# A planned attention and gated-MLP kernel: chunk 3's later score products added half to half, one denominator matmul for chunk 0, narrower last output pieces, and a new order

## The chip, the cores and the metric

The kernel runs on one core of one Trainium2 chip. Times are microseconds (us) on the device. The reported time is the median of several executions; one further execution was recorded by the profiler. An execution's time is a little longer than the span from the first to the last instruction that the profile shows.

The engines are named as the profile names them: PE multiplies matrices (PEld loads its weights), DVE works on vectors, ACT evaluates functions and copies out of PSUM, POOL and SP here mainly issue DMAs.

## The reference, cut to what matters

```python
h  = x + A(layernorm(x), wqkv, wo)           # x: [1, 2048, 512], bf16
h2 = h + B(layernorm(h), W_gate, W_up, W_down)

# A: 32 heads of 16, window of 8 keys at distance 0, 2, ..., 14 behind the query
logits = einsum("bhsd,bhswd->bhsw", q, kg) * scale     # masked where the key lies before position 0
attn   = softmax(logits, axis=-1)
o      = einsum("bhsw,bhswd->bhsd", attn, vg)
return o @ wo

# B: F = 1376
gate = relu(x @ W_gate);  up = x @ W_up
return (gate * up) @ W_down
```

## The kernel before

The 2048 rows go through in four chunks (0 to 3) of 512 columns. For each chunk a helper adds steps to a plan; each step has one engine, and a list `RANK` gives each step its place. `Plan.order` sorts every engine's steps by rank, so the list fixes the order in which each engine (and each DMA-issuing queue) takes its steps; steps of all four chunks are mixed. A step never overtakes another on its engine: when it waits, all behind it wait. `RANK` has one number per step in the order in which the steps are added, so a change that adds steps needs a new list.

The steps of one chunk `tk`, with the names used below:

- Layernorm of x: statistics (`xst`, `xag`, DVE, L467 and L470), Ln and Exp for the reciprocal root (ACT, L480, L484), normalising (L499 on ACT, L502 on DVE), transposing into columns by PE (L531, evacuated at L547) or by a transposing DMA on SP (L520, chunk 3).
- Projections q, k, v (PE, L572, four matmuls of 128x512 each; evacuated by ACT, L580).
- Products q*k: `pr` (DVE, L620, two head slices and four window positions in one instruction of 128x4096; chunk 0 in halves, L637). There are two half-windows hf = 0, 1, and for each two instructions, t = 0 and t = 2. One such tile has 8 slices of 512 columns: four window positions of head slice t, then the same four of slice t+1.
- Scores: `sc` (PE, L628). A matmul with the selector `sel` sums a head's elements over partitions, four of them side by side on 32 columns of the array. One `sc` step has 16 matmuls for the two tiles of a half-window. Then the exponential, `ex` (ACT, L696).
- Denominators: `den`. Chunks in `DEN1` first add the two half-windows' exponentials on DVE (`es`, L728) and use one matmul (L713); a chunk outside sums both in two matmuls (L716). Then Ln and Exp for the reciprocal (`dl`, `dr`, ACT, L719, L722). Chunks 1 to 3 multiply the weights by it early (`am`, DVE, L740).
- Broadcast of the weights to all elements of a head, `bd`: eight DMAs per chunk on SP (L756).
- Weighted values: `mu` (DVE, L788, 128x4096; chunk 0 in halves, L803), four per chunk, each followed by a tree of three additions. The first, 2048 wide, is an accumulating DMA issued on POOL for chunks 0 to 2 (`ta`, L831) and a DVE addition for chunk 3 (L791); the two others are on DVE (L791, L825).
- Output projection `wo0` to `wo3` (PE, L867), each needing all four trees; the residual (`rs`, DVE, L878; ACT for chunk 0), squares (ACT, L456), normalising (L502), transposes (PE, L531, or SP, L520).
- GLU: groups of four matmuls for up (`mmu`) and gate (`mmg`) per 128 features (PE, L940), evacuated by ACT (L944, L947), multiplied on DVE (`gu`, L968); the last 96 features go another way, in two tail groups (`mmT`, PE, L907; L913, L917).
- Down projection `dn` (PE, L990): 8 + 3 matmuls for 128 rows of output; then the residual (chunk 0 and 1: ACT copy L999 and accumulating DMA on POOL, L1024, `oa`; chunk 2 and 3: DVE, L1003) and the write (L1009, L1027, `os`). For chunk 3 the last 128 rows are done in column pieces cut at `LASTC`; the piece added last to the plan is written from ACT's queue, the others from SP's.

PSUM has eight banks of 128x512 in fp32, shared by all products of PE. PE begins with 56 matmuls on a zero tile (L421) and two smaller series of such (L429).

Of the kernel before, what the change touches and what calls it, by code (L numbers as in the profile page):

```python
# [17 lines left out]
RANK = [  # L18
# [38 lines left out]
]  # L57


# [33 lines left out]
class Plan:  # L93
# [9 lines left out]
    def add(self, key, *a, **k):  # L103
        op = Op(*a, **k)
        op.key = key
        op.seq = len(self.ops)
        if RANK:
            op.prio = RANK[op.seq]
        self.ops.append(op)
        for b in set(op.take) | set(op.use):  # L110
            b.left += 1
        return op
# [90 lines left out]
def kernel(  # L203
# [12 lines left out]
    Bsz, S, D = A_x.shape  # L216
# [5 lines left out]
    W = 8  # L222
    DIL = 2
    PADL = 16
    DEN1 = (1, 2, 3)
    BCD = {(0,0):"SSSS",(0,1):"SSSS",(1,0):"SSSS",(1,1):"SSSS",(2,0):"SSSS",(2,1):"SSSS",(3,0):"SSSS",(3,1):"SSSS"}
    PRE = ()
    PRD = ()
    PRH = {}
    ODA = (0, 1)  # L230
    LATE = "ud"
    NAB = 0
# [64 lines left out]
    V = nc.vector  # L297
# [94 lines left out]
    HSP = ()  # L392
    TMT = (0, 1, 2, 3)
    TTM, DTG, ATE = 0.0845, 0.35, 0.3
    LASTC = (D // 2,)

    LNA = ((0, 1, 0, 1), (0, 0, 0, 0))

# [156 lines left out]
    for tk in range(NCK):  # L555
# [50 lines left out]
        for hf in range(2):  # L606
            sc, ex = Buf(at_s), Buf(ex_s)
            scd, prd = [], []
            for t in range(0, NT, 2):
# [12 lines left out]

                hs = PRH.get((tk, hf, t))

# [62 lines left out]
            elif tk in MERGE:  # L687
                scd = [add(("sc%d" % hf, tk), "PE", (4 - sum((tk, hf, t) in PRH for t in (0, 2))) * MM + SW, lambda p=prd: [f() for _, _, f in p],
                           [a for a, _, _ in prd], apr, take=[sc], use=[b for _, b, _ in prd], lat=PEL)]
# [21 lines left out]
        def f_dn(exs=exs, dn=dn, tk=tk, es=None):  # L711
            if tk in DEN1:
                nc.tensor.matmul(dn.t[:], lhsT=(same if tk in EARLY else spread)[:], rhs=es.t[:], start=True, stop=True)  # L713
                return
            for hf in range(2):
                nc.tensor.matmul(dn.t[:], lhsT=(same if tk in EARLY else spread)[:], rhs=exs[hf].t[:], start=(hf == 0), stop=(hf == 1))  # L716
# [6 lines left out]

        if tk in DEN1:
            es = Buf(es_s)
# [250 lines left out]
        if tk == NCK - 1:  # L976
            cs = (0,) + LASTC + (D,)
            parts[-1:] = [(BPC - 1, a, b) for a, b in zip(cs, cs[1:])]
# [98 lines left out]
```

## Time and profile before

| | |
|---|---|
| median of 3 executions | 196.6 us (196.38 to 196.94) |
| profiled execution | 196.0 us |
| its span, first to last instruction | 193.7 us |
| PE busy | 188.5 us, 97% |
| DVE busy | 147.2 us, 76% |
| ACT busy | 115.2 us, 59% |
| POOL busy | 17.4 us, 9% |
| granted TensorE clock | 1.000 |

The profiled execution is 2.3 us longer than its span and 0.6 us shorter than the median. Busy time counts overlapping instructions once. A matmul of 128x512 shows a duration of 379 ns, but in a sequence the next one starts 216 ns after it, so lengths of sequences are read from the chain of waits, not from durations. The same holds, less strongly, for DVE and ACT.

### The profile page before, as it was taken

The numbers are of one execution on the slowest core, as the hardware profiler recorded it, in microseconds if no ns is written. First come the engines' busy times: TensorE is split into PE (matmuls) and PEld (weight loads), VectorE is DVE, ScalarE is ACT, GpSimd is POOL, SyncE is SP. The second block draws the span as 40 slices with busy tenths as digits, with TensorE's granted clock in tenths as the row PEclk, the third lists the DMA queues.
The fourth block names the chain that finished last, engine by engine and source line by source line (L and its number), as shares of the span: only waits on it lengthen the run. The fifth ranks groups of instructions, "written<-read, shape, count | busy, mean of one in ns | idle before, by whom it ended". The sixth has DMA issues, their size and how long they took to land.

```text
span 193.7 us, 3083 instructions
## 1 busy us (share of the span) xinstructions
PE 188.5 (97%) x1120; PEld 99.0 (51%) x1139; DVE 147.2 (76%) x239; ACT 115.2 (59%) x241; POOL 17.4 (9%) x35
## 2 busy tenths in 40 slices
PE   7999999999999999999999999999999999999993
PEld 7986455555436435454444554444445444545452
DVE  6889999999999999999997679999564401134331
ACT  3489898965999673965156649623478712435500
POOL 3000002330000013100044001003000000000000
PEclk9999999999999999999999999999999999999999
DMA  6799564999902609917579974135101624001102
GB/s 205 242 296 376 138 155 93 192 196 260 353 5 49 171 14 199 191 33 170 122 143 194 180 192 90 29 80 94 18 0 27 162 58 135 0 27 54 30 23 86
DMA packets 25070, 24.61 MB, mean 127 GB/s; under 512 B 11136, under 2 KB 21344, under 8 KB 25056
## 3 DMA queue, kind: packets, MB, share of 16 engines
q1 hardware_dynamic: 22032, 16.23, 30.1%
q0 software_dynamic: 2304, 7.34, 20.8%
q10 hardware_dynamic: 720, 0.85, 1.2%
q8 instruction: 9, 0.15, 0.3%
q14 instruction: 5, 0.04, 0.1%
HBM read 8.42 MB, written 2.10 MB: 54 GB/s over the span
## 4 chain that ended last, share of the span: by engine, by line
PE 97%; ACT 1%; issue 1%; DVE 0%; ACTq 0%
PE bank L940 35%; PE bank L572 21%; PE bank L990 20%; PE bank L867 7%; PE bank L628 4%; PE bank L421 3%; PE bank L907 3%; PE bank L531 2%; PE bank L429 1%; ACT up_sb L944 1%; PE bank L870 0%; PE bank L713 0%; PE bank L716 0%; DVE row L1003 0%; ACT vT L580 0%
## 5 line engine op out<-in xcount | busy, mean ns | idle before, releaser
L940 PE MATMUL bank<-quad,wgu_sb 128*128 128x512 bf16 x312 | 72.4, 379 | 0.4
L940 PEld LDWEIGHTS <-wgu_sb 128*128 128x128 bf16 x320 | 31.0, 98 | 36.4 <-issue 1.0
L990 PE MATMUL bank<-wd_sb,gT 128*128 128x512 bf16 (+2 forms) x185 | 39.6, 366 | 0.1
L944 ACT CAST up_sb<-bank 128x512 bf16<-128x512 f32 x40 | 22.3, 590 | 22.2 <-PE bank L940 20.5
L572 PE MATMUL bank<-quad,wqk_sb 128*128 128x512 bf16 (+1 forms) x148 | 29.4, 344 | 0.3
L947 ACT ACTIVATE gr<-bank 128x512 bf16<-128x512 f32 x40 | 23.5, 606 | 9.5 <-PE bank L940 5.2
L968 DVE TENSOR_TENSOR gT<-gr,up_sb 128x1024 bf16<-128x1024 bf16 x20 | 13.8, 688 | 19.4 <-ACT up_sb L944 10.5
L990 PEld LDWEIGHTS <-gT 128*128 128x128 bf16 (+1 forms) x187 | 18.2, 98 | 19.8 <-DVE gT L968 0.2
L620 DVE TENSOR_TENSOR big<-quad,kT 128x4096 bf16<-128x4096 bf16 x12 | 27.2, 2284 | 0.2 <-ACT kT L580 0.2
L788 DVE TENSOR_TENSOR big<-big,vT 128x4096 bf16<-128x4096 bf16 x12 | 27.1, 2285 | 0.2 <-PE bank L940 0.2
L572 PEld LDWEIGHTS <-wqk_sb 128*128 128x128 bf16 x152 | 16.7, 113 | 10.3 <-issue 0.2
L831 POOL DMA_DIRECT2D big<-big x12 | 10.5, 904 | 81.7 <-DVE big L788 54.2
L791 DVE TENSOR_TENSOR big<-big 128x1024 bf16<-128x1024 bf16 (+2 forms) x24 | 16.9, 728 | 0.0
L572 PE MATMUL bank<-quad,wv_sb 128*128 128x512 bf16 x61 | 15.3, 380 | 0.2
L867 PE MATMUL bank<-wo_sb,quad 128*128 128x512 bf16 x62 | 15.0, 379 | 0.1
L1003 DVE TENSOR_TENSOR row<-x_sm,bank 128x512 bf16<-128x512 bf16 (+1 forms) x9 | 5.5, 627 | 12.2 <-PE bank L990 12.2
L456 ACT ACTIVATE row<-x_sm,mv 128x512 bf16<-128x512 bf16 x12 | 8.6, 718 | 7.2 <-DVE mv L448 7.1
L547 ACT COPY quad<-bank 128x1024 bf16<-128x1024 bf16 (+1 forms) x10 | 8.6, 898 | 7.2 <-PE bank L531 7.2
L878 DVE SCALAR_TENSOR_TENSOR x_sm<-x_sm,bank 128x512 bf16<-128x512 bf16 x12 | 8.2, 687 | 4.9 <-PE bank L867 4.7
L580 ACT CAST kT<-bank 128x512 bf16<-128x512 f32 x16 | 9.1, 597 | 3.3 <-PE bank L572 1.8
L467 DVE BATCH_NORM_STATS2 st<-x_sm 128x6 f32<-128x512 bf16 x16 | 10.2, 675 | 0.4 <-DMA x_sm<-in_A_x_dram 0.4
L580 ACT CAST quad<-bank 128x512 bf16<-128x512 f32 x16 | 9.5, 602 | 1.6 <-PE bank L572 1.5
(77 smaller groups left out, 169.5 us busy)
## 6 DMA issues: line engine op xcount, KB each, us to landing
big<-big POOLq DMA_DIRECT2D x12, 512.0 KB, 5.3
big<-ex SPq DMA_DIRECT2D x32, 128.0 KB, 2.8
wgu_sb<-in_B_W_gate_dram SPq DMA_DIRECT2D x2, 688.0 KB, 7.7
wgu_sb<-in_B_W_up_dram SPq DMA_DIRECT2D x2, 688.0 KB, 7.5
wd_sb<-in_B_W_down_dram SPq DMA_DIRECT2D x2, 640.0 KB, 7.9
x_sm<-in_A_x_dram SPq DMA_DIRECT2D x2, 512.0 KB, 5.1
x_sm<-up_sb POOLq DMA_DIRECT2D x4, 256.0 KB, 3.8
out_dram<-x_sm SPq DMA_DIRECT2D x4, 256.0 KB, 2.3
```

What stands on the lines that cost most here:

```text
L572: nc.tensor.matmul(mm.t[:, lo:hi], lhsT=wv_sb[:, dt, t:D:NT] if c == 2 else wqk_sb[:, dt, c * D + t:(c + 1) * D:NT], rhs=xnT.t[:, dt, lo:h ...
L580: nc.scalar.copy(out=o, in_=mm.t[:])
L620: V.tensor_tensor(out=pb.t[:].rearrange("p (t w) s -> p t w s", t=2), in0=q4, in1=k4, op=ALU.mult)
L788: V.tensor_tensor(out=mt.t[:], in0=ab.t[:], in1=v8, op=ALU.mult)
L791: V.tensor_tensor(out=mt.t[:, 0:n, :], in0=mt.t[:, 0:n, :], in1=mt.t[:, n:2 * n, :], op=ALU.add)
L831: nc.gpsimd.dma_start(mt.t[:, 0:4, :], mt.t[:, 4:8, :], accum_op=ALU.add)
L867: nc.tensor.matmul(od.t[:], lhsT=OT.t[:, t, j * P:(j + 1) * P], rhs=wo_sb[:, t, :], start=(t == 0), stop=(t == NT - 1 and tk not in RPE))
L940: nc.tensor.matmul(mm.t[:fs, lo:hi], lhsT=wgu_sb[:, dt, g, ft * P: ft * P + fs], rhs=hnT.t[:, dt, lo:hi], start=(dt == 0), stop=(dt == NT ...
L944: nc.scalar.copy(out=ub.t[:fs, i, :], in_=um.t[:fs, :])
L947: nc.scalar.activation(out=gr.t[:fs, i, :], in_=gm.t[:fs, :], func=ACT.Relu)
L968: V.tensor_tensor(out=gt.t[:fs, 0:n, :], in0=gr.t[:fs, 0:n, :], in1=ub.t[:fs, 0:n, :], op=ALU.mult)
L990: nc.tensor.matmul(od.t[:, c0:c1], lhsT=gts[ft].t[:fs, ft % 2, j * P:(j + 1) * P], rhs=wd_sb[:fs, ft, c0:c1], start=(ft == 0), stop=(ft == ...
```

## The change

Four things are changed, and the list `RANK` with them:

1. `PRH` gets the two product tiles of chunk 3's second half-window. For each, a DVE step `ph` adds the tile's second half (slices 4 to 7) to its first half in place, 128x2048 long, and the score step then uses four matmuls for that tile and not eight: 8 in the step, not 16.
2. `DEN1` gets chunk 0: a DVE step `es` adds the two half-windows' exponentials, and one matmul replaces two.
3. `LASTC` is cut once more: the last 128 rows of output are done in pieces of 256, 128 and 128 columns, not 256 and 256. The plan has two matmul steps, one DVE step and one write more.
4. `RANK` has 751 entries, not 744, and another order throughout. What it moves, read from the sorted list, as far as the text below speaks of it:

| steps | before | after |
|---|---|---|
| chunk 0 `den` (PE) | after eight of chunk 1's projections | after four of them |
| chunk 0 `wo` (PE) | between chunk 1's two score steps | ahead of both, which then stand next to each other |
| chunk 3's second products `pr` (DVE) | one ahead of chunk 1's `wo`, one ahead of chunk 2's `mu` | both behind chunk 2's `mu`, with a `ph` behind each (other steps between) |
| chunk 3's second `sc` (PE) | ahead of chunk 1's GLU | in chunk 1's GLU, after 14 groups and both tail groups |
| chunk 3 `den` (PE) | in chunk 1's GLU, after 4 groups | two groups behind that `sc` |
| chunk 2 `wo` (PE) | after 15 groups and both tail groups of chunk 1's GLU | after 17 groups, both tail groups, that `sc` and that `den` |
| chunk 3 `es` (DVE) | ahead of chunk 2's last `mu` | between chunk 2's tree additions, ahead of the last two |
| chunk 3 `am` (DVE) | among chunk 2's tree additions | behind them and one `gu` |
| chunk 3 `wo` (PE), the first of the four | after 9 groups of chunk 2's GLU | after 14 groups and both tail groups of it |
| chunk 2 `dn` (PE) | among chunk 3's GLU groups | all ahead of chunk 3's GLU |
| chunk 0's first `oa` (POOL) | behind chunk 2's four `ta` | behind the first of them |
| W_down and W_up loads (SP) | down, up, up, down | down, down, up, up |
| last `dn` steps of chunk 3 (PE) | three full pieces, then the two of 256 columns | the ACT-queue piece of 128 first, mixed with three full pieces, then 256, then 128 columns |

```diff
@@ RANK: 744 numbers before, 751 after @@
...
-    DEN1 = (1, 2, 3)
+    DEN1 = (0, 1, 2, 3)
...
-    PRH = {}
+    PRH = {(3, 1, 0): 'V', (3, 1, 2): 'V'}
...
-    LASTC = (D // 2,)
+    LASTC = (D // 2, 3 * D // 4)
```

72 rows, old and new, of the table RANK are left out of this document.

## The prediction

> **What bounds the kernel now.** I read the page's busy shares and slices first, then the chain of waits.
>
> ```profile
> PE 188.5 (97%) x1120; PEld 99.0 (51%) x1139; DVE 147.2 (76%) x239; ACT 115.2 (59%) x241; POOL 17.4 (9%) x35
> PE   7999999999999999999999999999999999999993
> DVE  6889999999999999999997679999564401134331
> PE 97%; ACT 1%; issue 1%; DVE 0%; ACTq 0%
> L940 PE MATMUL bank<-quad,wgu_sb 128*128 128x512 bf16 x312 | 72.4, 379 | 0.4
> ```
>
> PE is full from the second slice to the last but one, and the chain that ended last is PE for 97%. So PE's own work sets the end: a matmul taken out counts in full, and a step on another engine counts only where PE comes to wait for it. The DVE row says where that is near: DVE too is at 9 until slice 22, and has room after it. A matmul of 512 columns lasts 379 ns; its pace stands in the chain (below: 16 in 3.46 us, 0.216 each), so its result comes about 0.16 us after the next one starts.
>
> The chain in order of time gives the lengths of what is changed (start, length, what):
>
> ```profile
> 29.48 0.43 PE bank L716 x2
> ...
> 33.36 0.67 PE bank L531 x12
> ...
> 54.33 0.98 PE bank L628 x16
> 55.31 0.34 PE bank L572
> ...
> 77.78 0.21 PE bank L713
> ...
> 99.19 3.46 PE bank L940 x16
> ...
> 113.68 2.37 PE bank L867 x11
> ...
> 130.96 6.69 PE bank L940 x31
> ...
> 146.51 0.66 PE bank L907 x8
> ...
> 181.11 9.56 PE bank L990 x55
> 190.66 0.02 issue
> 190.69 0.42 DVE row L1003
> ```
>
> **What PE loses and gains.** Chunk 0's two denominator matmuls take 0.43, the single one of another chunk 0.21: **-0.22**.
>
> A score step of 16 matmuls takes 0.98. They stand four abreast, so it is four rounds of 0.216, 0.86, and 0.12 that each such step costs besides. Two rounds go: **-0.43**. The bounds are 0.43 (the 0.12 stays whole) and 0.49 (half of all); I keep the first, since there is still one step. The matmul right behind a score step takes 0.34 and not 0.216, 0.12 more. After the change chunk 1's two score steps follow each other, so one such loss falls away: **-0.12**, with bounds 0 and 0.24 (both this and the 0.12 inside the step).
>
> The last piece of 256 columns becomes two of 128: 11 matmuls more, each half as wide. The 55 matmuls at the end take 9.56; 33 full ones by 0.216 make 7.13, so the 22 of 256 columns take 2.43, 0.110 each, 1.21 for eleven. The nearest row for 128 columns with new weights each time is the transposes: 12 in 0.67, 0.056 each. 22 of them make 1.23: **+0.02**. The Trainium skill ("TensorE: Matmul & The Clock Gate", section "Back-to-back issue gap") speaks against this edit: it gives about 81 ns, not 56, for a stream of weight loads and matmuls of 128 columns. By that the 22 would cost about 1.8 us, an estimate from that page; the transposes are such a stream and run at 56 ns, so the trace does not agree.
>
> **What the others gain.**
>
> ```profile
> L791 DVE TENSOR_TENSOR big<-big 128x2048 bf16<-128x2048 bf16 x4 | 4.8, 1218 | 0.0
> L1003 DVE TENSOR_TENSOR row<-x_sm,bank 128x512 bf16<-128x512 bf16 x7 | 4.6, 686 | 10.9 <-PE bank L990 10.9
> L728 DVE TENSOR_TENSOR row<-ex,ex 128x512 bf16<-128x512 bf16 x3 | 1.3, 419 | 0.0
> L1003 DVE TENSOR_TENSOR row<-x_sm,bank 128x256 bf16<-128x256 bf16 x2 | 0.8, 422 | 1.3 <-PE bank L990 1.3
> out_dram<-row SPq DMA_DIRECT2D x7, 128.0 KB, 1.7
> out_dram<-row SPq DMA_DIRECT2D x1, 64.0 KB, 1.5
> ```
>
> After the last matmul comes the addition of its piece. 256 columns take 0.42, 512 take 0.69; 128 should take 0.29: **-0.13**. The write behind it halves from 64 to 32 KB; from 128 to 64 KB a write lost only 0.2 of 1.7 us, so I count 0 and keep 0 to -0.1 for the range. (The next to last write is issued on the same queue more than half a microsecond earlier and does not hold it.) The piece written from ACT's queue is now finished first, well before the end.
>
> DVE gains two half-additions, 2 x 1.22, and one of 0.42 for chunk 0: 2.9 us. On DVE they cost that much; on PE they cost nothing as long as DVE's results are there when PE's order asks for them. This is the question of the forecast, and it is asked where DVE's slack is least.
>
> **The place that decides: chunk 2's trees and chunk 3's second scores, 94 to 117 us.**
>
> ```profile
> 80.00:100.00 20.00, 19.89 (x114) 9.47 (x115) 19.80 (x35) 10.65 (x25) 1.67 (x2) 1.00 0.57 119
> 100.00:118.00 18.00, 17.89 (x93) 8.87 (x93) 13.80 (x30) 11.48 (x25) 2.67 (x4) 1.00 0.91 180
> ```
>
> ```profile
> 93.12 1.38 DVE L502 TENSOR_SCALAR row<-x_sm,mv,rs 128x512 bf16<-128x512 bf16 x4
> 94.41 6.69 DVE L788 TENSOR_TENSOR big<-big,vT 128x4096 bf16<-128x4096 bf16 x3
> ...
> 103.55 0.68 DVE L791 TENSOR_TENSOR big<-big 128x1024 bf16<-128x1024 bf16 x1
> 104.27 0.42 DVE L825 TENSOR_TENSOR quad<-big 128x512 bf16<-128x512 bf16 x1
> ...
> 112.10 0.35 DVE L917 TENSOR_TENSOR row<-gr,bank 128x192 bf16<-128x192 bf16 x1
> 112.36 0.69 DVE L968 TENSOR_TENSOR gT<-gr,up_sb 128x1024 bf16<-128x1024 bf16 x1
> ```
>
> The columns of the stretches are PE, PEld, DVE, ACT, POOL busy, clock, DMA share, GB/s. DVE is busy 19.8 of 20 us up to 100, then 13.8 of 18: 4.2 us idle, more than the 2.9 added. First PE. It starts chunk 1's GLU at 99.19. In the new order the second score step has left the stretch ahead (-0.98), the denominator and the adjacent score steps give -0.22 and -0.12: 97.87. Then 14 groups of four matmuls (0.864) and two tail groups (0.66) run, 13.4 us, so PE asks for the halved products at 111.3.
>
> DVE ends chunk 1's normalising at 94.50. Its work up to the second half-addition then is: less two products that now come later (-4.4), `es` of chunk 0 (+0.4), four weighted values (8.8, a repeated one 2.2), two products (4.4), two half-additions (2.4), two tail steps (0.7), one tree end (1.1), one gate product (0.7): 108.6. The gate product may wait about 1 us for its group on PE. So DVE is some 2 us early.
>
> Then a round trip: the score step ends at 111.84; result 0.16 later; exponential 0.61; `es`, the last tree's two additions 0.42, 0.68, 0.42.
>
> ```profile
> 100.19 0.61 ACT L696 ACTIVATE ex<-bank 128x512 bf16<-128x512 f32 x1
> ...
> 104.14 0.62 ACT L719 ACTIVATE lnd<-bank 128x512 f32<-128x512 f32 x1
> ...
> 105.09 0.66 ACT L722 ACTIVATE rec<-lnd 128x512 bf16<-128x512 f32 x1
> ```
>
> That is 114.1. PE meanwhile has three groups and the denominator, 2.81 us, and comes to chunk 2's output projection at 114.65 (113.68 before). Slack 0.5 us. Behind the waiting `es` in DVE's order stand just these last additions, and PE's four `wo` steps wait for them: a delay in this loop is a stall of PE one to one. Chunk 0's `es` is hidden, as its denominator matmul can wait; chunk 0's reciprocal is used only after the trees.
>
> **Chunk 3's broadcast.**
>
> ```profile
> 60.28 5.11 SPq L756 DMA_DIRECT2D big<-ex  x8
> 106.24 8.66 SPq L756 DMA_DIRECT2D big<-ex  x8
> 117.85 2.28 DVE L788 TENSOR_TENSOR big<-big,vT 128x4096 bf16<-128x4096 bf16 x1
> 136.84 0.75 DVE L825 TENSOR_TENSOR quad<-big 128x512 bf16<-128x512 bf16 x2
> DMA to landing us min/median/max: 2.5/2.7/3.8
> DMA to landing us min/median/max: 2.6/4.0/7.0
> ```
>
> It now starts after the new den: 113.8, plus 0.16, 0.62, 0.66 and the weights' multiplication, 115.7 rather than 106.2. At the fast issue (5.11, last one landing 2.7 after it starts) it is complete at 122.9. DVE's work from 117.85 to 137.59 was 19.7; four normalisations (1.4) and one gate product now stand ahead, leaving about 17.8, so the trees end at 140.7. PE asks for them after 14 groups and two tail groups of chunk 2's GLU: 130.96 - 0.22 - 0.43 - 0.12 + 13.4 = 143.6. Slack 2.9 us. At the slow issue of before (under accumulating DMAs; 8.66) it would be 3.5 us later, and slack gone by 0.6. In the new order those DMAs were issued ten microseconds earlier, so I take the fast one. The one POOL transfer moved ahead of three tree additions and the load of W_up moved behind W_down both land microseconds before use.
>
> **The sum.** -0.22 - 0.43 - 0.12 + 0.02 - 0.13 = -0.88. With so many hand-overs at slack near 0.5 us I allow 0.1 of new waiting: -0.8. Profiled execution 196.0 (span 193.7) to 195.2; on the median 196.6 to **195.8**. From no change a measurement here can tell about 0.3%, 0.6 us.
>
> **Rivals.**
> (1) The loop through `es`, or a hand-over like it (chunk 0's and 1's `wo` are asked for within half a microsecond of their trees), is short by 0.3 to 1.2 us. For: PE waits in order for each. Against: before had hand-overs as close and the chain shows 97% PE. Time 196.1 to 197.0, mostly no change.
> (2) Matmuls of 128 columns run slower than the transposes: at three quarters of the 0.110 of 256 columns, 0.082 each, 22 cost 0.6 us more and 196.4 results. The page named above has this rule. Against: 0.056 in the chain.
> (3) Slower: chunk 3's broadcast is late. Place: PE stops ahead of chunk 3's `wo`. It decides once the eight take over 10 us instead of 7.2, and makes the kernel slower by 0.3% from 11.5 on. Before they took 10.8 (8.06 to the last issue and 2.7); with the 7.0 us landing of that stretch, 15. Midway, 13, the stall is 2.9 and the time 198.7; at 11.5 it is 197.2. For: it has been so slow. Against: the other DMAs of that stretch lie earlier now.
>
> **How the numbers follow.** Forecast 0.57, all of it faster. Rival 1 0.22 (0.18 no change, 0.04 slower). Rival 2 0.04, no change. Rival 3 0.17, slower, late trees of chunk 2 for the same cause counted in. Faster 0.57, same 0.22, slower 0.21. Range: all terms at their best ends, -0.22 - 0.49 - 0.24 + 0.02 - 0.13 - 0.1 = -1.16, and a little noise: 195.3; above, rival 1 whole and the near half of rival 3: 197.6. The forecast's own range is 195.4 to 196.0.
>
> **What would show it.** Right: PE busy about 187.7; one score step of 0.55 in the chain near 111; L716 gone, L713 four times; the 128-column matmuls of L990 0.056 apart; the last L1003 0.29; no wait of PE on DVE over 0.3. Wrong: a PE wait ahead of `wo` (L867) near 114 (rival 1) or near 143 with the broadcast's issue stretched beyond 8 us (rival 3); L990's last 22 matmuls over 1.5 us (rival 2). A stall anywhere else over 0.3 us would mean that the order's other hand-overs, which I took as covered, were not.

## The result, and the profile after

The changed kernel takes 195.06 us (median of 11 executions, 194.22 to 196.09); the kernel before 196.55 us (11 executions, 195.98 to 198.04). The ratio is 0.9922 with an interval of 0.9902 to 0.9943: faster by 0.8%. A second series (e1 below) gave 195.53 against 196.53, ratio 0.9957 (0.9927 to 0.9987). The direction was forecast; the first series' 195.06 lies below the range, which began at 195.3.

The profiled execution happens to be the longest of the 11: 196.09 us, span 194.2. Compared with the span of before, 193.7, it seems to show a loss. The chain in order of time tells why it is none (start, length, what):

```profile
1.66 5.15 DMA x_sm<-in_A_x_dram
...
8.41 4.03 DMA x_sm<-in_A_x_dram
...
19.37 1.05 PE bank L628 x16
...
27.48 0.22 PE bank L713
...
54.49 1.84 PE bank L628 x32
...
112.68 0.55 PE bank L628 x8
...
181.84 9.59 PE bank L990 x66
...
191.45 0.29 DVE row L1003
```

and the waits of PE (waiting line, releaser; us in total, times, longest):

```profile
PE bank L531 <- ACT row L499: 1.4, 1, 1.4
PE bank L421 <- DVE warm L322: 1.0, 1, 1.0
PE bank L572 <- ACT rs L480: 0.3, 1, 0.3
```

In this execution the chain runs over a second landing of input rows, at 12.4 us, and PE waits 1.4 us for them. That is ahead of everything the change touches. Two points are the same work in both kernels: the start of the first score step, and the start of the last addition. Of before, the first stands here, the second in the prediction:

```profile
17.99 0.98 PE bank L628 x16
```

So I divide an execution into four: the **start** (to the first score step), the **stretch** from there to the last addition, the **tail** from there to the end of the span, and the time **outside** the span.

- Before: start 17.99, stretch 172.70 (190.69 - 17.99), tail 3.01 (the span is 193.70), outside 2.3.
- Changed: start 19.37, stretch 172.08, tail 2.71 (194.16), outside 1.9.

Behind the start, what the diff did is there row by row: L716 is gone, a denominator takes 0.22 at 27.48; chunk 1's two score steps are one sequence of 32 matmuls; chunk 3's second step has 8 matmuls in 0.55 us; the 66 matmuls at the end take 9.59 (55 took 9.56); the last addition takes 0.29.

### The profile page after: what moved, and what is told of

It reads as the page before. It is cut to its first block, busy times and chain, and to the rows that moved or that the text cites. A ratio compares the mean times of both kernels' runs of the same rounds, so it can differ in the third digit from the quotient of the medians.

```text
span 194.2 us, 3099 instructions
## 1 busy us (share of the span) xinstructions
PE 188.5 (97%) x1141; PEld 98.3 (51%) x1141; DVE 150.7 (78%) x243; ACT 115.7 (60%) x241; POOL 17.0 (9%) x35
## 4 chain that ended last, share of the span: by engine, by line
PE 89%; DMA 5%; ACT 2%; issue 1%; DVE 1%; SPq 1%; ACTq 0%; POOL 0%
PE bank L940 36%; PE bank L990 20%; PE bank L572 17%; PE bank L867 7%; DMA x_sm<-in_A_x_dram 5%; PE bank L628 4%; PE bank L907 3%; PE bank L531 2%; ACT row L499 1%; DVE st L467 1%; SPq L336 1%; ACT quad L580 0%; PE bank L713 0%; PE bank L870 0%; ACT kT L580 0%
## 5 line engine op out<-in xcount | busy, mean ns | idle before, releaser
L990 PE MATMUL bank<-wd_sb,gT 128*128 128x512 bf16 (+3 forms) x198 | 39.1, 355 | 0.0
L1003 DVE TENSOR_TENSOR row<-x_sm,bank 128x512 bf16<-128x512 bf16 (+2 forms) x10 | 5.5, 579 | 10.7 <-PE bank L990 10.7
L502 DVE TENSOR_SCALAR row<-x_sm,mv,rs 128x512 bf16<-128x512 bf16 x24 | 8.6, 407 | 2.3 <-ACT rs L484 2.3
```

Of the source, the lines that this page charges most:

```text
L990: nc.tensor.matmul(od.t[:, c0:c1], lhsT=gts[ft].t[:fs, ft % 2, j * P:(j + 1) * P], rhs=wd_sb[:fs, ft, c0:c1], start=(ft == 0), stop=(ft == ...
```

## The experiments

Theories. **A**: the sum of the prediction holds, with PE never waiting behind the start. **B**: the new order, not the three edits, saves the time behind 20 us. **C**: the time outside the span depends on where an engine's stream of instructions ends, here that of GpSimd (POOL). **D**: the smaller last write shortens the end. This table holds all runs. The stretch and the tail are those of the one profiled execution, outside is the mean over all executions; GpSimd is how many instructions the trace records for that engine (the page's POOL row counts only the busy ones).

| kernel | GpSimd | stretch | tail | outside | median us | ratio to before |
|---|---|---|---|---|---|---|
| before, profiled first | 68 | 172.70 | 3.01 | 2.3 | | |
| e2, before again | 68 | 172.80 | 3.00 | 2.28 | 196.39 | 0.9997 (0.9979 to 1.0014) |
| e11, before + 9 | 77 | 172.75 | 3.01 | 1.78 | 195.83 | 0.9978 (0.9956 to 1.0) |
| changed | 65 | 172.08 | 2.71 | 2.05 | 195.06 | 0.9922 (0.9902 to 0.9943) |
| e1, changed again | 65 | 171.88 | 2.71 | 2.02 | 195.53 | 0.9957 (0.9927 to 0.9987) |
| e3, edits only | 69 | 174.8 | 3.09 | 1.81 | 197.70 | 1.0065 (1.004 to 1.009) |
| e4, order only | 64 | 172.49 | 3.00 | 2.05 | 196.55 | 0.9993 (0.9969 to 1.0017) |
| e5, no narrow pieces | 65 | 171.84 | 3.01 | 2.05 | 195.50 | 0.9963 (0.993 to 0.9996) |
| e6, changed + 3 | 68 | 171.87 | 2.71 | 2.27 | 195.22 | 0.9938 (0.9902 to 0.9974) |
| e7, changed + 4 | 69 | 171.89 | 3.10 | 1.84 | 195.39 | 0.994 (0.9908 to 0.9973) |
| e8, changed + 12 | 77 | 172.02 | 2.72 | 1.77 | 194.62 | 0.9909 (0.9877 to 0.9941) |
| e9, no half-additions | 65 | 172.30 | 2.73 | 2.01 | 195.35 | 0.9949 (0.992 to 0.9978) |
| e10, two denominator matmuls | 64 | 172.09 | 2.71 | 2.04 | 195.43 | 0.9953 (0.9923 to 0.9982) |

The four parts are not equally steady. Outside varies by 0.02 to 0.12 (standard deviation) from execution to execution of a kernel. The stretch differs by 0.1 between the three traces of the kernel before (e11 included; mean 172.75) and by 0.2 between the five of the changed kernel (e6 to e8 included; mean 171.95). The start is the noisy one, and with it the medians: in e1 the spans run from 192.2 to 194.7. Only profiled executions have a start that can be read; for the others an estimate is the mean span less stretch and tail. That gives 18.4 to 18.6 in the series of the old order and 18.4 to 19.0 in those of the new one, so no series shows that the new order shortens the start.

**e1 and e2, both kernels again, no edit.**

> The changed kernel itself, for a second profile. Its first profile was of its slowest execution: a wait of 1.4 us for input rows of chunk 1 before 20 us. Theory A (the sum of matmuls and the tail, -0.88, holds from the first score step to the end; the rest of the measured -1.5 lies ahead of that step, in the first 20 us, where executions differ): the first score step starts at 17.3 to 17.9, and from there to the last matmul it takes 172.1 again, as in the first profile, against 172.7 before. Theory B (the new order saves the rest behind 20 us): from the first score step to the last matmul it takes under 171.6. Time 0.990 to 0.994 of the kernel before by both.

> The kernel before, for a second profile: its first was one of its fastest executions. Ratio 1.000. Theory A: PE reaches the first score step later than 17.99, by 0.3 to 0.8 us in a usual execution, with a wait for ACT or for an input load there. Theory B: it reaches it at 18.0, and the time from there to the end is 173.0 or more.

The chain of e1, then that of e2:

```profile
1.69 4.69 DMA x_sm<-in_A_x_dram
...
18.29 0.98 PE bank L628 x16
...
111.40 0.55 PE bank L628 x8
...
114.86 3.45 PE bank L867 x16
...
190.17 0.29 DVE row L1003
```

```profile
1.69 4.72 DMA x_sm<-in_A_x_dram
...
18.32 0.98 PE bank L628 x16
...
191.12 0.42 DVE row L1003
```

Here the starts are equal, 18.29 and 18.32, and the kernels can be laid side by side: 0.95 of the difference is there when the last addition begins. For e1, A holds behind the start (its stretch is 171.88; B asked for under 171.6 up to the last matmul), but not ahead of it: the first score step comes at 18.29, not at 17.3 to 17.9. For e2 its theory A holds, with a start 0.3 later and no longer stretch. The stretch by engines (columns: stretch, its length, busy PE, PEld, DVE, ACT, POOL, clock, DMA share, GB/s), of e1 and then of e2:

```profile
18.29:190.17 171.88, 171.84 (x978) 84.20 (x978) 135.26 (x205) 104.36 (x217) 14.57 (x18) 1.00 0.50 113
```

```profile
18.32:191.12 172.80, 172.76 (x976) 84.02 (x976) 131.67 (x201) 103.86 (x217) 14.95 (x18) 1.00 0.50 112
```

PE idles 0.04 us in either: the saving is PE's own work, and DVE's 3.6 us more (2.9 were forecast) cost nothing. (In the trace of before used for the prediction 19 matmul records are missing, 1120 against 1139, so its PE busy time is read too low.)

**e3, the three edits on the order of before.** `RANK` is before's, with places for the added steps; with D = 512 the cuts of `LASTC` are those of the changed kernel.

```
-    DEN1 = (1, 2, 3)
+    DEN1 = (0, 1, 2, 3)
-    PRH = {}
+    PRH = {(3, 1, 0): 'V', (3, 1, 2): 'V'}
-    LASTC = (D // 2,)
+    LASTC = (256, 384)
```

> The half-additions, chunk 0's single denominator matmul and the two pieces of 128 on the order of before (each half-addition right behind its product, the sum right behind the mask, the last piece of each half in the changed kernel's sequence). Theory A: the sum without the adjacent score steps, -0.22 - 0.43 + 0.02 - 0.13 = -0.76 of 196.5, ratio 0.996, if DVE's 2.9 us more do not reach PE; the start is that of before. Theory B: the edits on the old order make PE wait for DVE, since both products stand ahead of chunk 1's and chunk 2's trees there: ratio 0.998 to 1.005.

It is slower than before, in the way that its theory B names and by a little more than that theory allowed (1.0065). The stretch by engines, the waits of PE in it, and rows of the chain:

```profile
17.70:192.49 174.79, 173.05 (x979) 83.74 (x978) 134.54 (x205) 104.02 (x217) 14.95 (x18) 1.00 0.50 114
```

```profile
PE bank L990 <- DVE gT L968: 1.0, 1, 1.0
PE bank L867 <- DVE quad L825: 0.3, 1, 0.3
PE bank L531 <- DVE row L502: 0.2, 1, 0.2
```

```profile
106.23 7.82 DMA big<-big
...
114.07 0.69 DVE big L791
...
115.49 3.41 PE bank L867 x15
```

PE stands still for 1.74 of 174.8 us: it waits for a gate product, for chunk 2's tree and for normalised rows, each done on DVE, where added steps now stand ahead of them, and two times for about 0.1 us. The tree was late for another reason too: DVE waited 1.95 us, up to 114.07, for the accumulating DMA of 7.8 us that is on the chain. The loss is larger than the idle time shows. The stretch is 2.0 longer than before's mean although PE has 0.63 less to do by the prediction's terms, which makes about 2.7. A matmul's shown duration, 379 ns with a pace of 216, covers 0.16 of each of the five waits, and that is most of the difference. The edits are a gain only under an order that gives DVE room. That this trace's waits come from the added DVE work and not from other differences of the order was not tried one by one.

**e4, the new order without the edits** (the constants of before).

> The new order without the three edits (no half-additions, two denominator matmuls for chunk 0, last pieces of 256 columns). Theory A: what the sum does not hold is in the order's first 20 us, so it gives the adjacent score steps and 0.5 to 0.8 us at the start: ratio 0.996 to 0.997. Theory B: the same size, but behind 20 us. If the order only makes room for the edits: ratio 1.000.

```profile
18.86 0.98 PE bank L628 x16
...
26.89 0.43 PE bank L716 x2
...
54.12 1.84 PE bank L628 x32
...
112.18 0.98 PE bank L628 x16
...
191.35 0.42 DVE row L1003
```

The stretch is 172.49, 0.26 less than before's 172.75, and the time is unchanged within the interval. The order saves the hand-over of chunk 1's adjacent score steps (1.84 in place of 2 x 0.98, and one slow matmul of 0.34 behind them less: 0.24) and nothing else in the stretch. B falls: the other 0.54 need the edits. A's 0.5 to 0.8 at the start did not come; the start of this execution is 18.86. The stretch and the time outside the span (2.05) are together 0.5 shorter than before's, and the median does not show it: that much the start can hide, and the interval still holds it.

**e9, the changed kernel without the half-additions** (`PRH = {}`), and **e10, with two denominator matmuls for chunk 0** (`DEN1 = (1, 2, 3)`), each in the new order.

> The changed kernel and its order, but chunk 3's q*k tiles are not added half to half, so that its second score step is again 16 matmuls. Theory A (the sum holds: TensorE never waits after 20 us): that step takes 0.98 where it took 0.55, so the stretch from the first score step to the last addition grows from 171.98 by 0.43 to 172.4, VectorE's busy time falls by 0.3 to 0.5 because two additions are gone, the rest of the execution (the tail of 2.74, and 2.03 outside the span) stays as in the changed kernel: about 195.7 where the changed kernel has 195.3. Theory B (the new order, and not the edits, saves what is saved behind 20 us): the stretch stays at 172.0 and the time at 195.3.

> The changed kernel and its order, but chunk 0's denominators come from two matmuls again. Theory A: the denominator step of chunk 0 takes 0.43 where it took 0.22, the stretch from the first score step to the last addition grows from 171.98 by 0.22 to 172.2, the rest stays as in the changed kernel: about 195.5. Theory B: the stretch stays at 172.0. A third way, that the additions on VectorE which the one matmul needs set the end of a wait, would show a stretch that does not grow or that shrinks.

The chains, first of e9, then of e10:

```profile
18.38 0.98 PE bank L628 x16
...
111.48 0.98 PE bank L628 x16
...
190.68 0.29 DVE row L1003
```

```profile
18.90 0.98 PE bank L628 x16
...
26.93 0.43 PE bank L716 x2
...
112.22 0.55 PE bank L628 x8
...
190.99 0.29 DVE row L1003
```

The steps have their old lengths again, 0.98 and 0.43. The stretches are 172.30 and 172.09, longer than the changed kernel's mean by 0.35 and 0.14 where A expected 0.43 and 0.22. That fits A within the 0.2 by which stretches of one kernel differ; alone, e10's is too small to tell. Taken singly, the order (0.26), the half-additions (0.35) and the denominator (0.14), less the 0.03 of the narrow matmuls, make 0.72 of the 0.80 by which the stretch is shorter. The medians (195.35 and 195.43 against 195.06 and 195.53) can't resolve such terms, because the start scatters by more.

**e5, the changed kernel with last pieces of 256 columns** (`LASTC = (256,)`).

> The changed kernel with the last 128 rows in two pieces of 256 columns again (the piece that stood first in its sequence stays first, the other is last). Sum: the last addition takes 0.42 again (+0.13), the last write lands some 0.1 later, the matmuls change by 0.02: from the start of the last addition to the end of the span 3.0 us, not 2.74, time +0.25 us on the changed kernel. The time outside the span (2.03 us for the changed kernel, 2.29 before) stays at 2.03 if it has nothing to do with the last write (theory C: it is the length of an engine's instruction stream), and goes to 2.29 if it is the smaller last write that shortens it (theory D).

```profile
180.56 9.56 PE bank L990 x55
...
190.14 0.42 DVE row L1003
```

The tail is 3.01, as before, and outside stays at 2.05, as in the changed kernel. So the narrow pieces are worth 0.3 of tail: 0.13 in the addition (0.42 to 0.29), 0.09 in the write behind it (from issue to landing 1.53 us at 64 KB, 1.44 at 32), and 0.07 from that landing to the end of the span (1.03 to 0.96). They do not change the time outside the span. D holds for the tail and falls for the time outside.

**e6, e7, e8: the changed kernel with 3, 4 and 12 more instructions on GpSimd**, made by cutting one or both of the zero fills of the padding at the start into more pieces; nothing else differs. **e11: the kernel before with 9 more.** For e6:

```
-        nc.gpsimd.memset(kT[:, :, 0:PADL], 0.0)
+        for t0, t1, c0, c1 in [(0, 1, 0, 16), (1, 2, 0, 16), (2, 3, 0, 16), (3, 4, 0, 16)]:
+            nc.gpsimd.memset(kT[:, t0:t1, c0:c1], 0.0)
```

> The changed kernel with three instructions more on POOL in the setup (one memset cut into four), 68 recorded instead of 65, the number of the kernel before. Theory C (the time outside the span goes by where POOL's instruction stream ends): the span as in the changed kernel, 192.2 to 194.7, the time outside it 2.29 as before. Theory D: 2.03, unchanged.

> Four instructions more on POOL, 69 recorded, as many as the edits on the old order had: there the time outside the span was 1.81 and POOL's last but one instruction came 0.45 us late. Theory C: the same here, a gap of 0.45 us ahead of POOL's last instructions and 1.81 outside. Theory D: 2.03 outside and no gap.

> Twelve instructions more on POOL, 77 recorded. Theory C: whatever POOL fetches at its end is now fetched earlier, while it is idle: 1.81 outside, no gap in the span, 0.2 us faster than the changed kernel. Theory D: 2.03 and no difference.

> The kernel before, with its two zero fills of the padding cut into eleven, so that GpSimd's stream has nine instructions more (77 in the trace, as many as in e8_pool_plus12, which had 1.77 us outside the span). Theory C (the time outside the span goes with where GpSimd's stream ends): 1.77 outside the span instead of 2.28, the stretch from the first score step to the last addition as before at 172.75, the tail 3.0: about 195.9 where the kernel before has 196.4. Theory D (the size of the last write sets it): 2.28 outside the span, 196.4 as before. By C, e8_pool_plus12 and this kernel differ by the span alone, by 1.0 to 1.1.

C is met in all four, also on the kernel before: with 68 instructions 2.27 and 2.28 outside, with 69 1.84 (and 1.81 in e3), with 77 1.77 and 1.78, with 64 or 65 2.01 to 2.05. With 69 a part only changes sides: in e3 and e7 GpSimd's last two instructions begin 0.44 us apart where all others have 0.08, so the tails are 3.09 and 3.10. Tail and outside together, for kernels with the narrow pieces: 4.73 to 4.76 with 64 or 65, 4.98 with 68, 4.90 and 4.94 with 69, 4.49 with 77. The medians of e6 and e7 (195.22 and 195.39) do not follow these terms; the start scatters by more.

What lies behind the counts is in the DMA records. The page's rows of the transfers that carry instructions, of after, and then of e8:

```profile
q8 instruction: 9, 0.15, 0.3%
q14 instruction: 5, 0.04, 0.1%
```

```profile
q8 instruction: 9, 0.15, 0.3%
q14 instruction: 6, 0.05, 0.1%
```

A sixth transfer of code on q14 (8 KB) appears within the span in e8 and e11 alone; it starts at 131 and 133 us, and PE does not wait there. In the other eleven traces that transfer is recorded behind the span's end: 1.8 to 1.9 us behind it with 64 or 65 instructions, 1.04 to 1.27 with 68, 0.6 with 69. For e1, from 190 us on (its span ends at 192.9), the row is

```profile
q14 instruction: 1, 0.01, 0.2%
```

So, as these records read, a stream that ends just short of a block of code leaves the fetch of the next block for the very end of the execution. The Trainium skill ("Runtime: NRT & Kernel Launch", section "Instruction fetch mechanics") says that each engine's code comes in blocks and that crossing into the next is mostly hidden; the trace agrees for the fetches inside the span, where PE idles 0.04 us in the whole stretch, and at the end it does not: between 68 and 77 instructions the same kernel's end differs by 0.5 us. Shown by the runs is that the end follows GpSimd's count; that the late fetch is the cause is read from the records. That GpSimd's code is what this queue moves is argued too, from the one transfer that shifts with its count. Why 68 costs 0.25 more than 65 isn't settled.

e8 is also the fastest version run, 194.62. With 77 instructions on both sides, e8 and e11, the change itself is worth 1.2 us by the medians and 1.0 by the means (194.92 and 195.92; the two ran in different series, in which before's medians were 196.42 and 196.35). The parts give 1.03: 0.73 in the stretch, 0.29 in the tail, 0.01 outside. Against the changed kernel as it was, e8's gain is 0.26 in tail and outside together; in the medians of e8 and e1, 194.62 and 195.53, there is more start in it than that.

## Why the prediction was right, and where it fell short

**What bounds the kernel.** Right: PE idles 0.04 of 172 us in the stretch, in both kernels, so each matmul taken out counted in full.

**The terms on PE.** -0.22, -0.43, -0.12 and +0.02 made -0.75; measured is 171.95 - 172.75 = -0.80. The denominator (0.43 to 0.22), the score step (0.98 to 0.55) and the narrow matmuls (9.56 to 9.59, so 22 of 128 columns in 1.24, 0.056 each) came as worked out. Rival 2 did not come. The 81 ns of the Trainium skill ("TensorE: Matmul & The Clock Gate", section "Back-to-back issue gap") do not hold for this stream either. Adjacent score steps were mis-sized: I took 0.12 and kept 0.24 as the bound; e4's stretch is 0.26 shorter, and in its chain the loss behind a score step and the one inside it both fall away (0.24).

**The hand-overs.** Right in place, without the 0.1 of new waits. In e1, whose start is 0.3 later than before's:

```profile
111.33 0.62 PE L628 MATMUL bank<-big,sel 128*32 128x512 bf16 x8
...
112.08 0.60 ACT L696 ACTIVATE ex<-bank 128x512 bf16<-128x512 f32 x1 [0.98 <-PE bank L628]
...
113.77 0.42 DVE L825 TENSOR_TENSOR quad<-big 128x512 bf16<-128x512 bf16 x1
...
114.70 3.62 PE L867 MATMUL bank<-wo_sb,quad 128*128 128x512 bf16 x16
115.33 0.76 DVE L740 TENSOR_TENSOR ex<-ex,rec 128x512 bf16<-128x512 bf16 x2 [0.46 <-ACT rec L722]
115.83 5.57 SPq L756 DMA_DIRECT2D big<-ex  x8
...
141.33 0.75 DVE L825 TENSOR_TENSOR quad<-big 128x512 bf16<-128x512 bf16 x2
143.44 0.74 PEld L867 LDWEIGHTS <-quad 128*128 128x128 bf16 x4
```

The last tree of chunk 2 ends at 114.19, half a microsecond ahead of its use at 114.70: the forecast slack, so rival 1 did not come. Chunk 3's broadcast is issued fast, 5.57 us (5.11 assumed), its trees end at 142.08 (140.7 forecast) and PE loads its weights at 143.44: 1.4 us to spare where 2.9 were forecast, and rival 3 did not come either. Of the 1.4 us that the trees are late, 0.9 are there when DVE can start on the first of them, at 123.81 in this trace where 122.9 was forecast, and 0.3 of these are e1's later start. One reading was loose: the prediction gave DVE room after slice 22, but its row is at 9 again in slices 25 to 28, about 116 to 136 us, where these trees begin. The order matters as much as feared: on the old one (e3) the same additions cost PE about 2.7 us.

**The tail.** Too small: -0.13 was counted, -0.29 measured. The addition gave the 0.13 that was counted; the write, set to 0 with a bound of -0.1, gave 0.09; and 0.07 lie between its landing and the end of the span, which the prediction did not count.

**The step that failed.** The sum went from span to execution by leaving the 2.3 us outside the span as they were. That put a term at nothing without a reason. It became 2.02 to 2.05: -0.25, which the prediction did not have, nor its range, whose low end used only the span's terms (-1.16). Stretch -0.80, tail -0.29 and outside -0.25 make -1.34, where the forecast was -0.8 and the best end -1.16. From 196.55, stretch and tail alone lead to 195.46, and with the term outside to 195.21, just below where the range began. The changed kernel has three GpSimd instructions less in its trace, 65 for 68 (the order alone, e4, has 64; the edits alone, e3, 69), and by e6 that alone moves the 0.25: three more zero fills restore 2.27. It is an effect of the count, not of the work saved. What is left of the first series' -1.49, 0.15, is put down to the start, by subtraction; no trace of those executions shows it. In the second series, with -1.00, the start went 0.34 the other way, and its 195.53 lies within the range. How far below the range the first median fell is chance, as far as the runs show.

**The signs in the profile** that I named were seen, but for one: PE's busy time, announced as 187.7, is 188.5 in the first trace and 187.9 in e1. It also counts what PE does ahead of the first score step, and that varies: the 56 matmuls on a zero tile took 5.7 us in the trace of before, 4.8 in the first trace of after and 4.6 in e1. Before's own figure was read low by the missing records (189.0 in e2).

## What to carry to other kernels

Where one engine is full, work moved off it counts in full, but only with an order that makes room on the engine that takes it: the same edits lost 0.65% in the old order and gained in the new one. Compare two traces between two points that both have, not by their spans: here the start moved by more than the change was worth, and the parts told what the medians could not. When less than 1% is at stake, look at the time outside the span too, and at the transfers that carry instructions: a handful of instructions more on an engine can move a fetch of code from the end of the execution into its middle.

## What was not expected of the hardware

- The time outside the span is no constant: it is 1.77 to 2.28 us here, and it changes between kernels that differ only in GpSimd's instructions (in the changed kernel, with 65, 68 and 77: 2.02, 2.27 and 1.77; in before, with 68 and 77: 2.28 and 1.78), and nothing in the tiles or their times shows it.
- The start follows the landing of input rows. In nine traces (e1, e2, e4, e5, e6, e8 to e11) the first score step begins 11.9 us after one landing of chunk 0's rows on the chain: 1.69 + 4.69 gives 18.29, 1.69 + 4.72 gives 18.32, and 5.26, 4.81 and 5.31 us of transfer (e4, e9, e10) give 18.86, 18.38 and 18.90. In the first trace of after, a second landing, of chunk 1's rows and 5.6 us later, set it instead and put it at 19.37.
